# Attention and two feed-forward stages on one core: the product with w_out as seven block products, one written order for all steps, and 29 matmuls in two halves

## The chip, the cores and the metric

The kernel runs on one core of a Trainium2 chip. TensorE (PE, its weight loads PEld), VectorE (DVE), ScalarE (ACT), GpSimd (POOL) and SyncE (SP, which issues the transfers) each work through a queue of their own in order and wait for each other by semaphores. The metric is the time of one execution on the device, in microseconds.

## What is computed

Attention for batch 2, 12 heads, 448 positions, 64 features a head, with a causal mask; its output, 896 tokens of 768 features, goes through two feed-forward stages. The weights arrive as 8-byte floats.

```python
x = attention(q, k, v)              # 896 x 768
g = maximum(x @ w_in, 0) ** 2       # w_in 768 x 2048
y = g @ w_out                       # w_out 2048 x 768
z = maximum(y @ w1, y @ w2, y @ w3) # each 768 x 768
out = z @ moe2_w_out                # 768 x 768
```

## The kernel before

Activations lie transposed: 128 features on the partitions, the 896 tokens in two halves (b = 0, 1, the two batches) of 448 columns. KDM = 6 blocks of 128 features make 768, KFF = 16 make 2048. Every f32 operand is split in two parts of the type fp32r, a rounded high part (`act_hi`, a ScalarE copy, L114) and the low rest (`dve_lo`, a VectorE subtraction, L117). A product of two blocks is three matmuls, high by high, high by low and low by high (`PASSES`), of 448 columns each.

The products with w_in and with w1, w2, w3 go by Winograd's form of Strassen's scheme (`Sevens`): a pair of column blocks of the weight, the two halves of the features and the two token halves make a 2 by 2 block product, done by seven products M1 to M7 in place of eight. Each of the seven is KH = 3 feature blocks by three passes, nine matmuls (L499). The operands are blocks of the activations (a11, a12, a22 and the sums s1 to s4) and of the weights (four blocks and four differences t1 to t4, by VectorE, L124). 8 pairs for w_in (`First`) and 9 for w1 to w3 (`Third`) make 1,071 matmuls. The product with w_out is an ordinary one (`out_slots`): 6 output blocks, 16 feature blocks, three passes, two token halves, 576 matmuls (L627).

A weight block comes by one transfer (`Weight.load`, L152, two buffers `wr`), a ScalarE cast of its upper bits (`cast`, L164) and a VectorE join (`join`, L169), which then issues the next load. `Quarter.hi` and `Quarter.lo` split three 128 by 128 pieces of it into one of five `wq` buffers.

The order of the work has two parts. Attention's twelve pairs of heads, 27 steps of the first weights (`k0` to `k26`) and the first four products (`u0` to `u3`) stand in a text, `ORDER`, one step after the other. Behind it a planner goes through the products as slots: beside each it puts the way out of the product before, the high and low parts of the slot three ahead (`LEAD`), and the weight steps by due times. The squares of the first stage are VectorE instructions (L518, L554).

Steps of the text, with the number of the pair behind the point: `s` scores (L347), `m` masked minimum on VectorE (L358), `e` exponential on ScalarE (L366), `r` reciprocals, `n` normalisation (L378) on POOL, or on VectorE with a stroke (n2'), `g` transposes (L386), `h` their copies to SBUF, on ScalarE, or on VectorE with a stroke, `w` product with v (L417), `xh`, `xl`, `xf`, `d1` to `d4`, `1h` to `4l` operands a and s of the first product. `2l.11` is the low part of s2 for the last pair, the last operand that M6 needs.

Of the kernel before, what the change touches and what calls it, by code (L numbers as in the profile page):

```python
# [32 lines left out]
w3.0 r2.2 n0.1 e5.2 s2.2 n3'.1 s0.3 m2.2 e4.2 m3.2 n2.1 g2.1 m1.3 r0.2 n1.2 e2.2 n6.2 g0.1 e3.2
m0.3 n5.2 h2'.1 g1.1 s2.3 s4.3 n0.2 e1.3 e0.3 m2.3 m3.3 h1.1 n4.2 m4.3 h0'.1 r1.2 s0.4 g3.2 e2.3
m5.3 s6.4 g3.1 xh.0 n2.2 e3.3 xl.0 g2.2 r2.3 n3.2 h3'.1 r1.3 n0.3 h3.2 m1.4 xf.0 s6.3 g0.2 m0.4
m6.3 g1.2 e5.3 w0.1 n3.3 n1.3 e4.3 k0 w1.1 w2.1 w3.1 m6.4 e6.3 s2.4 n2.3 h1.2 h2.2 h0.2 k1 r0.3
e0.4 m2.4 m3.4 n4.3 n5.3 s4.4 m4.4 s2.5 m5.4 e2.4 e6.4 e3.4 e4.4 e1.4 g2.3 n6.3 g1.3 e5.4 d3.1
g0.3 h2'.3 s6.5 m2.5 m3.5 r1.4 g3.3 n2.4 s4.5 m6.5 e2.5 n3.4 r2.4 s0.5 h1.3 w0.2 m4.5 r0.4 m1.5
# [1088 lines left out]
```

## Time and profile before

| | us |
|---|---|
| median of 3 runs | 464.23 (463.86 to 465.28) |
| the profiled execution | 468.29 |
| its span, first to last instruction | 466.5 |
| VectorE busy in the span | 364.3 |
| ScalarE busy in the span | 283.1 |

The profiled execution is one run under the hardware profiler. Durations of single instructions overlap with the start of the next on the same engine; the distance from one start to the next is what an instruction costs in a dense queue. A matmul of two f32 operands that are not split appears as two MATMUL records.

### The profile page before, as it was taken

The numbers are of one execution on the slowest core, as the hardware profiler recorded it, in microseconds if no ns is written. First come the engines' busy times: TensorE is split into PE (matmuls) and PEld (weight loads), VectorE is DVE, ScalarE is ACT, GpSimd is POOL, SyncE is SP. The second block draws the span as 40 slices with busy tenths as digits, with TensorE's granted clock in tenths as the row PEclk, the third lists the DMA queues.
The fourth block names the chain that finished last, engine by engine and source line by source line (L and its number), as shares of the span: only waits on it lengthen the run. The fifth ranks groups of instructions, "written<-read, shape, count | busy, mean of one in ns | idle before, by whom it ended". The sixth has DMA issues, their size and how long they took to land.

```text
span 466.5 us, 6969 instructions
## 1 busy us (share of the span) xinstructions
PE 460.7 (99%) x2434; PEld 402.0 (86%) x2434; DVE 364.3 (78%) x813; ACT 283.1 (61%) x609; POOL 42.4 (9%) x90
## 2 busy tenths in 40 slices
PE   8999999999999999999999999999999999999997
PEld 5766676899999999899999999999999999999996
DVE  5999999998888899992322272898888988898963
ACT  5999999756555557952323254566457656665541
POOL 3656455000000000000000000000000000000000
PEclk9999999999999999999999999999999999999999
DMA  6463543223344441435323423342256466400014
GB/s 214 138 219 127 173 161 91 69 73 112 96 127 136 137 135 45 136 108 186 98 84 112 136 74 111 131 135 68 91 182 197 147 199 203 136 1 1 34 52 152
DMA packets 47619, 56.28 MB, mean 121 GB/s; under 512 B 1761, under 2 KB 43873, under 8 KB 47585
## 3 DMA queue, kind: packets, MB, share of 16 engines
q1 hardware_dynamic: 47296, 55.61, 37.0%
q8 instruction: 19, 0.31, 0.3%
q10 hardware_dynamic: 288, 0.23, 0.2%
q14 instruction: 16, 0.12, 0.1%
HBM read 53.08 MB, written 2.75 MB: 120 GB/s over the span
## 4 chain that ended last, share of the span: by engine, by line
PE 96%; DVE 3%; issue 0%; DVEq 0%
PE ps L499 47%; PE ps L627 26%; PE ps L752 7%; PE ps L347 7%; PE ps L386 4%; PE ps L417 4%; PE ps L1014 1%; PE ps L962 1%; DVE pr L358 1%; DVE s L124 0%; DVE pr L378 0%; DVE a L117 0%; DVE wd L169 0%; DVE st L374 0%; DVE wq L117 0%
## 5 line engine op out<-in xcount | busy, mean ns | idle before, releaser
L499 PE MATMUL ps<-s,wq 128*128 128x448 f32 x612 | 129.6, 368 | 0.0
L499 PEld LDWEIGHTS ps<-s,wq 128*128 128x128 f32 x612 | 114.8, 188 | 11.7 <-ACT s L509 0.2
L499 PE MATMUL ps<-a,wq 128*128 128x448 f32 x459 | 100.0, 370 | 0.0
L627 PE MATMUL ps<-gh,wq 128*128 128x448 f32 x384 | 95.3, 368 | 0.0
L499 PEld LDWEIGHTS ps<-a,wq 128*128 128x128 f32 x459 | 85.5, 188 | 9.0 <-issue 0.4
L117 DVE TENSOR_TENSOR wq<-wd,wq 128x384 fp32r<-128x384 f32 (+1 forms) x87 | 46.0, 533 | 49.3 <-ACT wq L114 45.0
L627 PEld LDWEIGHTS ps<-gh,wq 128*128 128x128 f32 x384 | 72.1, 188 | 7.3
L114 ACT CAST wq<-wd 128x384 fp32r<-128x384 f32 (+1 forms) x87 | 42.9, 499 | 53.8 <-PE ps L627 33.1
L164 ACT CAST up<-wr 128x768 f16<-128x768 bf16 (+1 forms) x58 | 60.8, 1049 | 7.1 <-DMA wr<-in_moe_w 2.1
L169 DVE SCALAR_TENSOR_TENSOR wd<-wr,up 128x768 int32<-128x768 int32 (+1 forms) x58 | 53.8, 928 | 6.1 <-ACT up L164 5.4
L627 PE MATMUL ps<-gl,wq 128*128 128x448 f32 x192 | 55.2, 368 | 0.0
L509 ACT COPY s<-ps 128x448 f32<-128x448 f32 x51 | 27.1, 533 | 37.6 <-PE ps L499 37.1
L366 ACT ACTIVATE pr<-pr,st 128x384 f32<-128x384 f32 (+3 forms) x84 | 44.1, 529 | 5.4 <-DVE st L358 5.2
L117 DVE TENSOR_TENSOR wq<-wt,wq 128x384 fp32r<-128x384 f32 x68 | 37.2, 551 | 9.4 <-ACT wq L114 9.1
L114 ACT CAST wq<-wt 128x384 fp32r<-128x384 f32 x68 | 34.3, 515 | 16.5 <-DVE wt L124 13.4
L378 POOL TENSOR_SCALAR pr<-pr,st 128x256 f32<-128x256 f32 (+3 forms) x77 | 39.9, 534 | 37.6 <-DVE st L374 22.7
L627 PEld LDWEIGHTS ps<-gl,wq 128*128 128x128 f32 x192 | 36.0, 188 | 3.6
L358 DVE CUSTOM_DVE_ANT_0 pr<-ps,mask 128x384 f32<-128x384 f32 (+3 forms) x84 | 34.5, 443 | 5.5 <-PE ps L347 4.9
L347 PE MATMUL ps<-k,q 64*128 64x128 f32 (+3 forms) x168 | 35.5, 445 | 0.0
L386 PEld LDWEIGHTS ps<-ident,pr 128*128 128x128 f32 x192 | 21.6, 140 | 7.5 <-issue 3.1
L386 PE MATMUL ps<-ident,pr 128*128 128x128 f32 x192 | 26.3, 276 | 0.3 <-DVE pr L378 0.3
L124 DVE TENSOR_TENSOR s<-ps,s 128x448 f32<-128x448 f32 (+1 forms) x31 | 18.2, 598 | 9.4 <-ACT s L509 4.5
(108 smaller groups left out, 494.0 us busy)
## 6 DMA issues: line engine op xcount, KB each, us to landing
wr<-in_moe_w_out SPq DMA_DIRECT2D x18, 768.0 KB, 4.3
wr<-in_moe_w SPq DMA_DIRECT2D x18, 768.0 KB, 4.3
wr<-in_moe_w_in SPq DMA_DIRECT2D x16, 768.0 KB, 4.7
v<-in_v SPq DMA_DIRECT2D x12, 256.0 KB, 4.6
wr<-in_moe_w_out SPq DMA_DIRECT2D x6, 512.0 KB, 3.5
q<-in_q SPq DMA_DIRECT2D x11, 256.0 KB, 2.7
out<-s SPq DMA_DIRECT2D x14, 192.0 KB, 1.9
k<-in_k SPq DMA_DIRECT2D x11, 224.0 KB, 2.9
```

The source lines that it names most:

```text
L114: nc.scalar.copy(hi, src)
L117: nc.vector.tensor_tensor(out=lo, in0=src, in1=hi.bitcast(F32), op=SUB)
L164: nc.scalar.copy(self.up.bitcast(FH)[:, :, 1::2], self.top)
L169: nc.vector.scalar_tensor_tensor(out=self.t.bitcast(I32), in0=self.rest, scalar=13, in1=self.up.bitcast(I32), op0=ALU.logical_shift_right, ...
L347: nc.tensor.matmul(sc[:, :keys[w]], self.n["q"][r, w // 2 * P:(w // 2 + 1) * P], self.n["k"][r, :keys[w]], start=True, stop=True,)
L358: nc.vector.tensor_tensor_reduce(out=self.pr[:, offs[u]:offs[u] + n], in0=self.sc[u][:, :n], in1=mask[:, mask.shape[1] - n:], scale=-SCALE ...
L366: nc.scalar.activation(sl, sl, ACTF.Exp, bias=self.st[:, 0, u:u + 1], scale=-1.0, accum_out=self.st[:, 1, u:u + 1],)
L378: engine.tensor_scalar(sl, sl, self.st[:, 2, u:u + 1], 1.0, op0=ALU.mult, op1=ALU.mult)
L386: nc.tensor.transpose(pt[:, i], self.pr[:, offs[u] + kc * P:offs[u] + (kc + 1) * P], shared["ident"])
L499: nc.tensor.matmul(self.acc[n], self.q[n].t[:, ew, i], X[OPERANDS[n]][i][:, ex], start=n in ("M1", "M2", "M5") and i == 0 and e == 0, stop ...
L627: nc.tensor.matmul(acc[b], quarter.t[:, ew, f - k0], (gh, gl)[ex][f][0][:, b], start=f == 0 and e == 0, stop=f == KFF - 1 and e == 2, skip ...
L752: nc.tensor.matmul(acc, a, b, start=start and i == 0 and e == 0, stop=i == KH - 1 and e == 2, skip_group_check=True,)
```

## The change

1. The product with w_out becomes a seven-product scheme as well (`Second`): 8 pairs of feature blocks (j), the two column halves of w_out (l and r, 3 blocks each) and the two token halves. Products run M1, M2, M6, M5, M7, M4, M3, each over j = 0 to 7, three column blocks by three passes. M1 of j 0 to 3 and M3 of j 4 to 7 take one unsplit f32 matmul in place of the three passes (`FULL`). The weight differences (`T1` to `T4`) and activation sums (`S1` to `S4`) are made per j; the activation operand of each product and j is split by `XH` (ScalarE) and `XL` (VectorE). w_out comes in 16 blocks of 768 KB in place of 12 of 768 and 6 of 512.
2. The planner, slots and due times go. `ORDER` now holds 1,693 steps, from the first score to the last results of the w1 to w3 product: `C` cast and `J` join of a weight block, `H` and `L` high and low part of a quarter, `T` differences, `M1` to `M7` products, `V0`, `V1` and so on the way out. The text of attention is another one too: up to `2l.11` it has 25 normalisations on VectorE where the old one has 7 (of 84), 6 joins for 4, 7 `T` steps for 5, 7 `L` steps for 7.
3. In the first and third products, from the third pair on, M1 is copied by ScalarE into the PSUM bank of M2, which adds to it there; VectorE's addition goes (`fresh`). The square of the first stage is done by ScalarE, relu and then square.
4. One matmul in each `Sevens` group (M6, second block, second pass: 17) and 12 in the w_out product are taken as two of 224 columns (`matmul_in_parts`): 29.
5. `st` has three buffers for two. The work behind `ORDER`, with the last product, stays but for how buffers are returned.

```diff
--- before.py
+++ after.py
-LEAD = 3
+FULL = dict(M1=(0, 1, 2, 3), M3=(4, 5, 6, 7))
 RING = 5
 OWN, MORE = 29, 18
-BESIDE = 4
 
 ORDER = """
-s0.0 m0.0 s2.0 m1.0 m2.0 e0.0 s4.0 s6.0 e1.0 m3.0 e2.0 m4.0 e3.0 m5.0 m6.0 s6.1 s0.1 e4.0 r1.0
...
-2l.7 h0.11 3l.9 g1.11 u0.2 1l.7 k23 g2.11 xf.10 u2.2 h1.11 u1.2 h2.11 w0.11 w1.11 k18 k21 k19 k24
-w2.11 k26 k25 w3.11 v1.0 v2.0 u3.0 u3.1 u3.2 d2.11 d4.11 2h.11 d1.11 2l.11 xh.11 4h.11 1h.11 xl.11
-1l.11 4l.11
+s0.0 m0.0 m1.0 s2.0 s4.0 m2.0 e1.0 m3.0 m4.0 s6.0 e0.0 m5.0 e2.0 m6.0 e4.0 e5.0 r2.0 s6.1 s0.1
...
+xh'.7 m6.10 g1.9 g0.9 e2.10 n6.9 xl.7 s4.11 s2.11 h0'.9 3h.5 h1.9 e1.10 m2.11 h2.9 e4.10 C.i3 w0.8
+w1.8 r1.10 m3.11 r2.10 L.f1M2 w2.8 w3.8 g3.9 m5.11 M1a.f0 n2.10 n3'.10 e6.10 g1.10 M1b.f0 m4.11
+e5.10 s6.11 xh.8 d1.7 xl.8 J.i3 H.f1M1 e2.11 M1c.f0 r0.10 n5.10 e5.11 xf.8 h3.9 m6.11 n6'.10 s0.11
+m0.11 w0.9 V0.f0M1 3l.5 e6.11 e3.11 h1.10 m1.11 w1.9 w2.9 e0.11 n1.10 n0'.10 L.f0M2 e4.11 n4.10
+w3.9 g3.10 L.f1M1 M1a.f1 r1.11 1h'.7 g2.10 n2.11 r0.11 n4.11 C.i4 g0.10 n3'.11 h2.10 T1.f0 M2a.f0
+T2.f0 J.i4 e1.11 n6'.11 r2.11 h3.10 n5.11 d3.9 T1.f1 H.f0M6 M1b.f1 M2a.f1 M2b.f0 4l.3 g1.11 g0.11
+n1'.11 L.f0M6 h0.10 w0.10 C.i5 w1.10 J.i5 T2.f1 n0.11 2h.7 T3.f0 w2.10 w3.10 3h.9 h1.11 g3.11
+g2.11 xh.10 xl.10 h0.11 M2b.f1 M2c.f0 M1c.f1 1l.7 h3.11 T3.f1 T1.f2 d4.7 h2.11 xf.10 w0.11 H.f1M6
+2l.7 w1.11 H.f1M3 w2.11 L.f1M6 w3.11 M2c.f1 4h.7 C.i7 L.f1M3 d2.11 2h'.11 V0.f1M1 2l.11 H.f0M7
+4l.7 more d1.11 xh.11 L.f0M7 H.f0M5 J.i7 M6.f0 1h'.11 3l.9 M6.f1 V0.f0M6 1l.11 M7.f0 L.f0M5 H.f1M7
+T4.f0 C.i6 H.f1M5 L.f1M7 L.f1M5 H.f0M4 V0.f1M6 J.i6 C.i11 T4.f1 M5.f0 M5.f1 H.f3M1 d4.11 L.f0M4
+4h.11 M7.f1 V0.f1M2 V0.f0M7 V1.f1M2 J.i11 xl.11 H.f1M4 V0.f1M7 T1.f3 V2.f1M2 L.f1M4 M4.f0 L.f3M1
...
+T3.o1 V1.f4M3 T2.o1 M3.f6 V1.f6M2 V0.f6M3 V0.f7M2 H.o3M2 S2.o2 L.o3M2 M3.f7 V0.f7M4 J.o3r V1.f7M4
+V1.f6M4 S4.o1 V2.f4M3 V1.f7M2 M1.o2 L.o6M1 M2.o0 V0.f7M3 XH.o6M1 XL.o4M6 S1.o1 XH.o1M7 V1.f6M3
+H.o1M2 XL.o6M1 C.o4r M1.o3 H.o4M1 V2.f6M7 J.o4r L.o4M1 T1.o4 M1.o4 XH.o0M5 V2.f6M3 L.o1M2 M2.o1
...
+WL.5 Z4.l V.2
...
-                self.st = att.tile([P, 3, 2 * NQ + 1], F32, tag="st", name="st")
+                self.st = att.tile([P, 3, 2 * NQ + 1], F32, tag="st", name="st", bufs=3)
...
+    def matmul_in_parts(acc, w, x, at, **flags):
+
+        for c in (slice(0, at), slice(at, S)):
+            if c.start < S:
+                nc.tensor.matmul(acc[:, c], w, x[:, c], skip_group_check=True, **flags)
...
+                    matmul_in_parts(
                         self.acc[n], self.q[n].t[:, ew, i], X[OPERANDS[n]][i][:, ex],
-                        start=n in ("M1", "M2", "M5") and i == 0 and e == 0,
-                        stop=i == KH - 1 and e == 2, skip_group_check=True,
+                        S // 2 if (n, i, e) == ("M6", 1, 1) else S,
+                        start=n in self.starts and i == 0 and e == 0, stop=i == KH - 1 and e == 2,
...
         def e1(self):
-            return [lambda: self.keep("s1")], []
+            if self.fresh:
+                return [lambda: self.keep("s1")]
+            return [lambda: nc.scalar.copy(self.d, self.b)]
...
+        def relu(self, f, b, acc=None):
+            o = unit_of(g, "g", f, b, 2)
+            nc.scalar.activation(o, o if acc is None else acc, ACTF.Relu)
+
+        def square(self, f, b):
+            o = unit_of(g, "g", f, b, 2)
+            nc.scalar.activation(o, o, ACTF.Square)
+
+        def squared(self, f, b, acc=None):
+
+            return [lambda: self.relu(f, b, acc), lambda: self.square(f, b)]
 
         def c11(self):
             o = self.fa, 0
-            return [lambda: self.added(*o, self.d, "s1")], [lambda: square(unit_of(g, "g", *o))]
+            if self.fresh:
+                return [lambda: self.added(*o, self.d, "s1"), *self.squared(*o)]
+            return self.squared(*o, self.d)
...
+    class Second:
+
+
+        B = [ps[i][:, :S] for i in (6, 7, 0)]
+        C = [ps[i][:, :S] for i in (2, 4, 3)]
+        HALF = KH * P
+
+        X_AT = dict(M1=(0, 0), M2=(1, 0), M5=(0, 0), M7=(0, 1), M4=(1, 1), M3=(1, 0))
+
+        W_AT = dict(M1=(0, 0), M2=(0, 1), M5=(0, 0), M7=(1, 0), M4=(0, 1), M3=(1, 1))
...
+        def t_1(self, j):
+            dve(self.wt("M5", j), self.wt("M7", j), self.wt("M1", j), SUB)
+
+        def t_2(self, j):
+            t = self.t2[j] = s_tile()[:, :self.HALF].rearrange("p (m c) -> p m c", c=P)
+            dve(t, self.wt("M3", j), self.wt("M5", j), SUB)
+
+        def t_3(self, j):
+            dve(self.wt("M7", j), self.wt("M3", j), self.wt("M7", j), SUB)
+
+        def t_4(self, j):
+            dve(self.wt("M4", j), self.wt("M2", j), self.t2[j], SUB)
+
+        def s_3(self, j):
+            dve(self.g(j, 0, 1), self.g(j, 0, 0), self.g(j, 0, 1), SUB)
+
+        def s_2(self, j):
+            k = "pair", j // 2
+            if k not in self.s2:
+                self.s2[k] = Kept("s2", 6, (2, S))
+            self.s2[j], self.s2[j, "kept"] = self.s2[k].t[:, j % 2], self.s2[k]
+            dve(self.s2[j], self.g(j, 1, 1), self.g(j, 0, 1), SUB)
+
+        def s_1(self, j):
+            dve(self.g(j, 0, 0), self.s2[j], self.g(j, 0, 0), ADD)
+            self.s2[j, "kept"].used()
+
+        def s_4(self, j):
+            dve(self.g(j, 1, 0), self.g(j, 1, 0), self.s2[j], SUB)
+            self.s2[j, "kept"].used()
+
+        def x_hi(self, n, j):
+            self.x[n, j] = units.take("x")
+            act_hi(self.x[n, j][0][:, 0], self.xt(n, j))
+
+        def x_lo(self, n, j):
+            t = self.x[n, j][0]
+            dve_lo(t[:, 1], self.xt(n, j), t[:, 0])
+            self.x_used(n, j)
+
...
+        def acc(self, n, m):
+            return (self.C if n in ("M2", "M5", "M3") else self.B)[m]
+
+        def flags(self, n, j, first, last):
+            return dict(
+                start=n in ("M1", "M2", "M5") and j == 0 and first, stop=j == NI - 1 and last,
+            )
+
+        def run(self, n, j):
+            (x, key), q = self.x[n, j], self.q[n, j]
+            for m in range(KH):
+                for e, (ew, ex) in enumerate(PASSES):
+                    matmul_in_parts(
+                        self.acc(n, m), q.t[:, ew, m], x[:, ex],
+                        S // 2 if (j % 4, m, e) == (0, 1, 1) else S,
+                        **self.flags(n, j, e == 0, e == 2),
+                    )
+            units.give(key)
+
+        def run_full(self, n, j):
+            for m in range(KH):
+                nc.tensor.matmul(
+                    self.acc(n, m), self.wt(n, j)[:, m], self.xt(n, j), skip_group_check=True,
+                    **self.flags(n, j, True, True),
                 )
-
-                def run(quarter=quarter, k0=k0 + r0, k1=k0 + r1):
-                    for f in range(k0, k1):
-                        for e, (ew, ex) in enumerate(PASSES):
-                            for b in range(B):
-                                nc.tensor.matmul(
-                                    acc[b], quarter.t[:, ew, f - k0], (gh, gl)[ex][f][0][:, b],
-                                    start=f == 0 and e == 0, stop=f == KFF - 1 and e == 2,
-                                    skip_group_check=True,
-                                )
-                    if m == KDM - 1:
-                        for f in range(k0, k1):
-                            units.give(gh[f][1])
-                            units.give(gl[f][1])
-
-                res.append(Slot(run, quarter, None, (m, k0 + r0)))
-
-        def evac():
-            if m == KDM - 1:
-                shared["y"] = acc
-                return [], []
-            y[m] = units.take(f"y{m}", F32)
-            return [lambda b=b: nc.scalar.copy(y[m][0][:, b], acc[b]) for b in range(B)], []
-
-        res[-1].evac = evac
-        return res
-
-    blocks_o = [Weight(w_o, f, 1, 0, DM) for f in range(KF2)]
+            self.used(n, j)
+            self.x_used(n, j)
+
+        def out(self, n):
+            def at(m, h, b):
+                return unit_of(y, "y", m + h * KH, b, 2 + h)
+
+            def kept(h, b):
+                return [lambda m=m: nc.scalar.copy(at(m, h, b), self.B[m]) for m in range(KH)]
+
+            def added(h, b):
+                return [lambda m=m: dve(at(m, h, b), self.C[m], at(m, h, b), ADD) for m in range(KH)]
+
+            return dict(
+                M1=kept(0, 0), M2=added(0, 0), M6=kept(1, 0), M5=[], M7=kept(1, 1) + added(1, 1),
+                M4=kept(0, 1), M3=added(1, 0),
+            )[n]
...
```

## Rows read from the trace of the kernel before

**Rows 1.** Page, busy time by engine, then groups: line engine op, out<-in, count, busy, mean ns

```profile
span 466.5 us, 6969 instructions
...
PE 460.7 (99%) x2434; PEld 402.0 (86%) x2434; DVE 364.3 (78%) x813; ACT 283.1 (61%) x609; POOL 42.4 (9%) x90
...
L378 POOL TENSOR_SCALAR pr<-pr,st 128x256 f32<-128x256 f32 (+3 forms) x77 | 39.9, 534 | 37.6 <-DVE st L374 22.7
...
L386 PE MATMUL ps<-ident,pr 128*128 128x128 f32 x192 | 26.3, 276 | 0.3 <-DVE pr L378 0.3
```

**Rows 2.** Windows, attention and each product: from:to, length, busy by engine, clock, DMA

```profile
10.00:91.10 81.10, 80.77 (x570) 56.33 (x570) 78.23 (x298) 75.34 (x232) 39.45 (x76) 1.00 0.45 145
91.10:186.00 94.90, 94.90 (x461) 86.13 (x460) 82.51 (x149) 55.37 (x99) 0.00 (x0) 1.00 0.35 106
186.00:306.00 120.00, 120.00 (x582) 108.77 (x581) 63.84 (x102) 57.05 (x98) 0.00 (x0) 1.00 0.35 115
306.00:420.00 114.00, 114.00 (x554) 103.52 (x553) 101.52 (x186) 70.04 (x126) 0.00 (x0) 1.00 0.42 138
420.00:466.50 46.50, 43.05 (x244) 42.16 (x242) 33.32 (x63) 20.06 (x42) 0.00 (x0) 1.00 0.17 60
```

**Rows 3.** Chain of waits in order of time, from 88 us: start, us, what

```profile
88.73 95.08 PE ps L499 x459
183.81 3.65 PE ps L627 x18
187.46 2.03 PE ps L499 x9
189.49 3.72 PE ps L627 x18
193.21 1.86 PE ps L499 x9
195.07 111.60 PE ps L627 x540
306.67 113.46 PE ps L499 x549
...
434.77 28.30 PE ps L752 x162
```

**Rows 4.** Timeline of PE, 183 to 188 us: start, us, what

```profile
183.64 0.57 PE L627 MATMUL ps<-gh,wq 128*128 128x448 f32 x2
...
186.89 0.57 PE L627 MATMUL ps<-gh,wq 128*128 128x448 f32 x2
```

**Rows 5.** Timeline of the weight loads, 181 to 188 us

```profile
181.72 0.90 PEld L499 LDWEIGHTS ps<-s,wq 128*128 128x128 f32 x5 [0.18 <-ACT s L509]
...
187.35 0.71 PEld L499 LDWEIGHTS ps<-a,wq 128*128 128x128 f32 x4 [0.28 <-ACT s L509]
```

**Rows 6.** Timeline of PE, three places in attention

```profile
42.54 0.92 PE L347 MATMUL ps<-k,q 128*128 128x448 f32 x2
43.30 1.04 PE L386 MATMUL ps<-ident,pr 128*128 128x128 f32 x8
...
76.44 0.60 PE L386 MATMUL ps<-ident,pr 128*128 128x128 f32 x4
...
90.62 7.60 PE L499 MATMUL ps<-s,wq 128*128 128x448 f32 x36
```

**Rows 7.** Timeline of VectorE, three places

```profile
70.88 0.68 DVE L378 TENSOR_SCALAR pr<-pr,st 128x256 f32<-128x256 f32 x1
71.48 0.15 DVE L373 TENSOR_SCALAR st<-st 128x2 f32<-128x2 f32 x1
...
81.20 0.34 DVE L378 TENSOR_SCALAR pr<-pr,st 128x256 f32<-128x256 f32 x1
81.46 0.38 DVE L443 CAST s<-s 128x448 fp32r<-128x448 f32 x1
...
90.51 0.62 DVE L117 TENSOR_TENSOR s<-s,s 128x448 fp32r<-128x448 f32 x1
91.05 0.62 DVE L117 TENSOR_TENSOR a<-ps,a 128x448 fp32r<-128x448 f32 x1
...
97.50 0.55 DVE L117 TENSOR_TENSOR wq<-wd,wq 128x384 fp32r<-128x384 f32 x1
97.97 0.55 DVE L124 TENSOR_TENSOR wt<-wd 128x384 f32<-128x384 f32 x1
...
98.97 0.95 DVE L169 SCALAR_TENSOR_TENSOR wd<-wr,up 128x768 int32<-128x768 int32 x1
99.84 0.55 DVE L117 TENSOR_TENSOR wq<-wt,wq 128x384 fp32r<-128x384 f32 x1
```

**Rows 8.** Timeline of ScalarE, high halves of two weight quarters

```profile
102.15 0.51 ACT L114 CAST wq<-wt 128x384 fp32r<-128x384 f32 x1
102.57 0.51 ACT L114 CAST wq<-wd 128x384 fp32r<-128x384 f32 x1
```

**Rows 9.** Page, DMA issues: count, KB each, us to landing

```profile
wr<-in_moe_w_in SPq DMA_DIRECT2D x16, 768.0 KB, 4.7
```

**Rows 10.** Timeline of POOL, 69 to 83 us

```profile
70.45 3.33 POOL L378 TENSOR_SCALAR pr<-pr,st 128x384 f32<-128x384 f32 x6 [2.84 <-DVE st L373]
78.19 2.68 POOL L378 TENSOR_SCALAR pr<-pr,st 128x384 f32<-128x384 f32 x5 [4.41 <-DVE st L374]
```

More of the change, by code (lines that the diff above doesn't have):

```diff
@@ L33 @@
[L33 to L38, printed above, removed]
@@ L124, in dve, with load_next @@
         nc.vector.tensor_tensor(out=o, in0=a, in1=b, op=op)
+    todo, blocks, line = {}, {}, []
+    def load_next():
+        if line:
+            line.pop(0).load()
     class Kept:
@@ L660, in tile_attention_moe_moe, with c12, c21 @@
[L660 to L664 removed]
+            return [
+                lambda: self.keep("s3"), lambda: self.added(self.fb, 1, self.c, "s3"),
+                *self.most(self.fb, 1, "s3"),
+            ]
+        def c12(self):
+            return [lambda: self.added(self.fb, 0, self.c, "s2"), *self.most(self.fb, 0, "s2")]
+        def c21(self):
+            return [lambda: self.whole(self.fa, 1, self.b)]
@@ L839, in way_out @@
-    def way_out(n):
-        prior = slots[n - 1] if n else None
-        return prior.evac() if prior is not None and prior.evac else ([], [])
-    def beside(n):
-        before, late = way_out(n)
-        if n in urgent:
-            before = before + [urgent[n]]
-        for step in before + weight_steps(n) + late + extra.get(n, []):
-            step()
-        units.settle()
-    def convert(f):
-        t, key = g[f]
-        gh[f], gl[f] = units.take(f"gh{f}"), units.take(f"gl{f}")
-        hi_lo(gh[f][0], gl[f][0], t)
-        units.give(key)
@@ L992, in tile_attention_moe_moe @@
-    more = ctx.enter_context(tc.tile_pool(name="more", bufs=1))
-    units.add(more, MORE, "m")
-    for e in range(2):
-        todo[f"v{BESIDE - 1}.{e}"]()
-    for n in range(BESIDE, len(slots)):
-        slots[n].run()
-        beside(n)
-    before, late = way_out(len(slots))
-    for step in before + late:
-        step()
+    own = ExitStack()
+    att = own.enter_context(tc.tile_pool(name="att", bufs=2))
+    constants(att)
+    prs = [att.tile([P, offs[-1]], F32, name=f"pr{n}", bufs=1) for n in range(PR)]
@@ new lines, in tile_attention_moe_moe, with more_units @@
+    warm = att.tile([P, 2 * P], FR, name="warm", bufs=1)
+    nc.vector.memset(warm.bitcast(F32), 0.0)
+    for _ in range(WARM):
+        nc.tensor.matmul(ps[7][:, :2 * P], warm[:, :P], warm, start=True, stop=True)
+    for t in prs:
+        nc.gpsimd.memset(t[:, offs[-2] + S:], 0.0)
+    def more_units():
+        own.close()
+        units.add(ctx.enter_context(tc.tile_pool(name="more", bufs=1)), MORE, "m")
+    todo["wload"], todo["more"] = load_next, more_units
+    for i in range(B * NP):
+        todo |= Pair(i).steps()
@@ new lines, in tile_attention_moe_moe @@
+    order = ORDER.split()
+    line += [blocks[n[2:]] for n in order if n.startswith("C.")]
+    for i in range(3):
+        todo[f"load.{i}"]()
+        if i:
+            todo[f"loadv.{i - 1}"]()
+    done = set()
+    for n in ORDER.split():
+        assert n not in done or n == "wload", n
+        done.add(n)
+        todo[n]()
+        step, *i = n.split(".")
+        if step == "s0" and int(i[0]) + 3 < B * NP:
+            todo[f"load.{int(i[0]) + 3}"]()
+        if step == "w0" and int(i[0]) + 2 < B * NP:
+            todo[f"loadv.{int(i[0]) + 2}"]()
```

586 lines of the change are left out of this document (281 added, 305 removed).

## The prediction

> **What bounds the kernel now.** I read the page's busy line first [rows 1]: PE is busy 99% of the span, but that share can't be taken as it stands, because matmuls overlap in the records. The table by stretches [rows 2] splits the run into attention (to 91.1 us), the product with w_in (to 186), the product with w_out (to 306), the products with w1 to w3 (to 420) and the last product. The reader is to see two regimes. In attention VectorE is busy 78.23 of 81.10 us and ScalarE 75.34, so VectorE sets the pace. From 91.1 to 420 PE never stops, while VectorE falls as low as 63.84 of 120 us beside w_out. The granted clock is 1.00 (the 2.4 GHz level) in every stretch.
>
> The chain of waits [rows 3] confirms it: from 88.73 us on it is PE's own matmuls, piece after piece, so a matmul removed there shortens the end by its start distance, as long as the other two engines keep up. The w_out product is three pieces, 18 + 18 + 540 matmuls: 3.65 + 3.72 + 111.60 = 118.97 us. The large piece gives 111.60/540 = 206.7 ns per matmul of 448 columns; the third product's piece, 113.46/549, gives the same.
>
> **The w_out product.** Before: 576 matmuls, 118.97 us. After: 8 pairs of feature blocks, 7 products, 3 column blocks, 168 places. 144 of them take three passes, 432 matmuls: 432 x 206.7 ns = 89.3 us. The other 24 (M1 of j 0 to 3, M3 of j 4 to 7) are unsplit f32. Such a matmul appears as two MATMUL records; the unsplit 448-column score starts at 42.54 and PE's next work at 43.30 [rows 6], so 0.76 us each, 24 x 0.76 = 18.2 us. (Three passes would be 0.62 us: these 24 cost PE 3.3 us and spare the other engines the splitting.) Sum 107.5 us: **11.4 us less** on the path that sets the end.
>
> **The 29 split matmuls.** No row has 224 columns with this operand type. Lower bound: the line through 448 columns (206.7) and 384 (28.30/162 = 174.7 ns) [rows 3] reaches 95 ns at 224, so a split would give back 17 ns, 0.5 us in all. Upper bound: each half costs what 384 columns do, so 143 ns more per split, 4.1 us. Nearest for a short matmul with its own weight load are the transposes of 128 columns, four in 0.60 us with 276 ns taken by one, so (0.60 - 0.28)/3 = 0.11 us apart [rows 1, 6]; I take 115 ns a half, 23 ns more per split, **+0.7 us**. The Trainium skill ("TensorE: Matmul & The Clock Gate", Back-to-back issue gap) gives N/2.4 + 2.5 ns: for 448 columns 189 ns, where this trace has 206.7, so the measurement decides; by that page, as an estimate, the 29 splits would cost under 0.1 us.
>
> **Two paces.** The same 448-column matmul also runs at another distance. Between 183.64 and 186.89 us 16 matmuls start, 203 ns each [rows 4], and this holds from one wait of the weight loads (0.18 us at 181.72) to the next (0.28 us at 187.35) [rows 5]; behind the second the pace is 206.7 again for the rest of the stage. The clock is the same, so the pace looks like a state that a jolt in the stream of loads can set, and it then lasts. A split is a jolt: two loads where one was, one in 51 of the remaining matmuls. Lower bound 0; upper bound all 1,467 remaining three-pass matmuls (1,035 of the first and third products, 432 here) at 203: 1,467 x 3.6 ns = 5.3 us. One jolt of two led to the faster pace; I take half, **-2.6 us**.
>
> **Attention, in the new order.** M6.f0 is the first product for which attention must be over; it waits for VectorE's step `2l.11`. Before, it starts at 90.62 us [rows 6], and the step is the 448-column difference at 90.51 [rows 7]. I count VectorE's steps up to `2l.11` in both orders. A step costs the distance to the next start in dense work [rows 7]: 448 columns 0.54 us (90.51 to 91.05), 384 columns 0.47 (97.50 to 97.97), a join 0.87 (98.97 to 99.84). New: 18 more normalisations on VectorE (25 for 7), 2 more joins (6 for 4) +1.7, 2 more T differences +0.9, one more placement +0.5; fewer copies of x and sums on VectorE -1.8; `d1`, `d4`, `3l.9`, `4l.7` moved behind -2.2. A normalisation of 256 columns took 0.26 us (81.20 to 81.46) where POOL was idle and 0.60 (70.88 to 71.48) where POOL ran the same operation beside it [rows 7, 10]. So 18 cost between 4.7 and 10.8 us, and the whole is +3.8 to +9.9 us. POOL was busy 39.45 of 81.1 us [rows 2] and loses 18 of its 77 normalisations [rows 1], so most new ones should find it idle; and VectorE had 2.9 us idle that another order may fill. I take **+5 us**. The Trainium skill ("SBUF — State Buffer", Who interferes with whom) says that VectorE in a two-port mode and GpSimd share a port pair and that whoever issues second is fully blocked; the pair 0.26 and 0.60 agrees.
>
> **Who must keep up behind it.** Behind `2l.11` I count, with the same prices, 278 us of VectorE work to the end of the order against 326 us of PE work, and 212 us of ScalarE (0.42 us for a high half) [rows 8]. The squares go from VectorE to ScalarE, whose 57.05 of 120 us leave room. So the cover for all new T, S, XH and XL steps is PE's own stream; without it each would cost its 0.47 to 0.54 us. But one stretch is tight. From M2.o0 to M4.o0 (M2, M6, M5, M7 of w_out) VectorE has 69 L and XL steps, 30 T, 15 S, 9 joins and 6 others, 67.5 us, against 69.2 us of matmuls, and at M2.o0 it can be ahead by little: the last results of the w_in product, which it handles in that place, leave PE only one product, M1.o2 (2.3 us), before it. VectorE did 101.52 of 114 us (89%) beside a full PE [rows 2], where it had no need of more. Bounds: 0 (it keeps up, with that lead) and 67.5/0.89 - 69.2 = 6.6 us. I take **+1.5 us**, nearer to zero because it reached 96% in attention, where it was needed.
>
> **Loads.** Per block SP issues one transfer, as before, behind the join that frees the buffer; two buffers, 4.7 us to landing [rows 9]. Eight blocks of the left half must now be decoded by the end of the w_in product. From each join to the cast two blocks later I count the matmuls in the order: mostly 5.6 us and more; 1.9 for `i13`, 2.3 for `b2`, 3.7 for four others. There ScalarE waits up to 2.8 us, with high halves for products some five places later queued behind it. I take nothing, since ScalarE is at two thirds; without that cover 2.8 us each.
>
> **Sum.** The profiled execution took 468.29 us with a span of 466.5; the median of the runs is 464.23, 0.9% less, and both get the same differences. -11.4 + 0.7 - 2.6 + 5 + 1.5 = -6.8: 464.2 - 6.8 = **457.4 us**. All low ends together: -11.4 - 0.5 - 5.3 + 3.8 = -13.4, 450.8, or 448 if VectorE's idle 2.9 us in attention are filled too; all high ends: -11.4 + 4.1 + 9.9 + 6.6 = +9.2, 473.4.
>
> **Rivals.**
> 1. The fast pace holds nearly everywhere. For: it lasted until the next wait. Against: one jolt of two ended it. 457.4 - 2.7 = 454.7; with a good attention order 450. Chance 0.20.
> 2. The splits do nothing for the pace, and attention costs its full 9.9: 464.2 - 11.4 + 0.7 + 9.9 + 1.5 = 464.9, no change that can be measured (0.3%, 1.4 us, is about what a measurement of this kernel can tell). For: VectorE is at 96% there. Against: POOL has less to do. Chance 0.08.
> 3. The other side: VectorE becomes the bound. One mechanism, its steps at the upper prices above: 0.60 us for a normalisation up to `2l.11`, and 89% at most between M2.o0 and M4.o0, where PE then waits for XL steps. 464.2 - 11.4 + 0.7 + 9.9 + 6.6 = 470.0, slower. It decides once VectorE's delays together pass 11.4 - 0.7 + 1.4 = 12.1 us. For: 98% load in that stretch. Against: attention's 96%, and the order places most XL steps well ahead of their products. Chance 0.12.
> 4. The change doesn't do what it says: seven products for eight bring nothing, because 24 unsplit f32 matmuls cost more than 0.76 us. It would take 1.2 us each; no row speaks for that. Under 0.02, counted with 3.
>
> **Numbers.** Forecast (452 to 462) 0.60, rival 1 0.20, rival 2 0.08, rival 3 with 4 0.12. Faster: 0.60 + 0.20 and a quarter of rival 2, 0.82; the same 0.06; slower 0.12. Range 449 to 464.5: it leaves out the slow end of rivals 2 and 3 and the best end of rival 1.
>
> **What would show it.** The w_out matmuls in about 107 us plus any waits; pieces of the chain at 203 and at 207 ns, and a change of pace at a split; M6.f0 starting at 94 to 97 us instead of 90.6; VectorE above 94% beside M2 to M7 of w_out, ScalarE near two thirds. Wrong, if PE idles for VectorE by more than 3 us there, if M6.f0 starts before 91 or after 101, or if the pace is below 200 or above 210 ns.

## The result, and the profile after

The changed kernel takes 458.54 us (median of 4 runs, 457.79 to 459.29); the kernel before, in the same series, 464.52 (463.86 to 465.28). The ratio is 0.9857, 95% interval 0.9816 to 0.9898: faster by 6.0 us (1.4%). 457.4 was forecast, in a range of 449 to 464.5. The profiled execution took 458.93 us, with a span of 457.1.

The page's busy line, in the form of [rows 1]:

```profile
PE 447.7 (98%) x2367; PEld 385.1 (84%) x2367; DVE 396.3 (87%) x900; ACT 324.3 (71%) x712; POOL 35.2 (8%) x72
```

VectorE works 32 us more than before, ScalarE 41 us more, and the end still comes earlier: most of it lies beside PE. The table by stretches, with the columns of [rows 2]: attention, the products with w_in, w_out and w1 to w3, the last product, and then the tight stretch from M2.o0 to M4.o0:

```profile
10.00:94.70 84.70, 82.29 (x567) 56.36 (x567) 82.18 (x309) 78.81 (x237) 32.69 (x59) 1.00 0.51 157
94.70:187.80 93.10, 92.38 (x460) 84.22 (x459) 75.82 (x136) 78.07 (x150) 0.00 (x0) 1.00 0.59 170
187.80:298.70 110.90, 110.90 (x520) 95.51 (x519) 108.18 (x203) 79.67 (x153) 0.00 (x0) 1.00 0.36 108
298.70:418.40 119.70, 119.44 (x597) 109.74 (x596) 98.26 (x181) 66.34 (x126) 0.00 (x0) 1.00 0.26 85
418.40:457.10 38.70, 34.73 (x199) 34.09 (x197) 26.95 (x53) 16.59 (x36) 0.00 (x0) 1.00 0.20 72
197.80:266.30 68.50, 68.50 (x342) 62.54 (x341) 67.03 (x129) 49.40 (x96) 0.00 (x0) 1.00 0.34 104
```

The table shows two things. Beside w_out VectorE is busy 108.18 of 110.90 us, and in the tight stretch 67.03 of 68.50 (98%), with PE busy all the time. And attention is longer: 84.7 us from 10 us on, where it was about 80.6 [rows 2, 6].

The chain of waits, in order of time (start, us, what), to be held against [rows 3]:

```profile
150.62 4.43 DMA wr<-in_moe_w_out
155.13 1.07 ACT up L250
...
160.12 27.82 PE ps L558 x137
187.94 4.51 PE ps L814 x12
192.45 3.64 PE ps L558 x18
196.09 2.25 PE ps L814 x6
...
202.44 78.64 PE ps L558 x397
...
301.41 5.70 DMA wr<-in_moe_w
...
310.46 92.21 PE ps L558 x457
```

L558 is a three-pass matmul, L814 an unsplit f32 one (two records each): a product of three takes 2.25 us, 0.75 us each. The large piece holds 377 whole matmuls and the 20 halves of ten split ones; 78.64/387 = 203 ns each, where [rows 3] had 206.7. The timeline of PE gives the start of M6.f0:

```profile
94.70 4.47 PE L558 MATMUL ps<-s,wq 128*128 128x448 f32 x23
```

94.70 us, where [rows 6] had 90.62.

### The profile page after: what moved, and what is told of

Read it like the earlier page. It is cut to its first block, busy times and chain, and to the rows that moved or that the text cites. A ratio compares the mean times of both kernels' runs of the same rounds, so it can differ in the third digit from the quotient of the medians.

```text
span 457.1 us, 6969 instructions
## 1 busy us (share of the span) xinstructions
PE 447.7 (98%) x2367; PEld 385.1 (84%) x2367; DVE 396.3 (87%) x900; ACT 324.3 (71%) x712; POOL 35.2 (8%) x72
## 4 chain that ended last, share of the span: by engine, by line
PE 53%; DVE 9%; DMA 2%; ACT 2%; issue 0%; ACTq 0%; SPq 0%
PE ps L558 46%; PE ps L989 5%; PE ps L814 2%; DVE z L202 1%; DMA wr<-in_moe_w 1%; DVE y L202 1%; DVE piece L195 1%; DVE wd L202 1%; DVE wd L255 1%; DMA wr<-in_moe_w_out 1%; DVE s L195 1%; ACT up L250 1%; ACT wq L192 1%; DVE s L202 0%; DVE z2l L195 0%
## 5 line engine op out<-in xcount | busy, mean ns | idle before, releaser
L558 PE MATMUL ps<-s,wq 128*128 128x448 f32 (+1 forms) x629 | 130.1, 362 | 0.6 <-ACT ps L596 0.6
L558 PEld LDWEIGHTS ps<-s,wq 128*128 128x128 f32 x629 | 115.1, 188 | 11.1 <-ACT ps L596 1.0
L558 PE MATMUL ps<-a,wq 128*128 128x448 f32 x459 | 101.6, 370 | 0.7 <-ACT wq L192 0.3
L558 PEld LDWEIGHTS ps<-a,wq 128*128 128x128 f32 x459 | 85.2, 188 | 10.3 <-DVE wq L195 0.8
L558 PE MATMUL ps<-x,wq 128*128 128x448 f32 (+1 forms) x444 | 89.0, 362 | 0.0
L558 PEld LDWEIGHTS ps<-x,wq 128*128 128x128 f32 x444 | 81.5, 188 | 6.9 <-issue 0.6
L250 ACT CAST up<-wr 128x768 f16<-128x768 bf16 x56 | 60.2, 1075 | 12.0 <-DMA wr<-in_moe_w_in 3.8
L192 ACT CAST wq<-wd 128x384 fp32r<-128x384 f32 x91 | 46.0, 511 | 26.3 <-PE ps L558 26.1
L255 DVE SCALAR_TENSOR_TENSOR wd<-wr,up 128x768 int32<-128x768 int32 x56 | 53.7, 959 | 9.4 <-ACT up L250 9.4
L195 DVE TENSOR_TENSOR wq<-wd,wq 128x384 fp32r<-128x384 f32 x91 | 49.0, 551 | 9.3 <-ACT wq L192 9.0
L440 ACT ACTIVATE pr<-pr,st 128x128 f32<-128x128 f32 (+3 forms) x84 | 44.0, 528 | 6.9 <-DVE st L432 6.6
L432 DVE CUSTOM_DVE_ANT_0 pr<-ps,mask 128x128 f32<-128x128 f32 (+3 forms) x84 | 34.8, 444 | 4.5 <-PE ps L421 4.2
L421 PE MATMUL ps<-k,q 64*128 64x384 f32 (+3 forms) x168 | 36.0, 446 | 1.5 <-DVE st L432 1.3
L591 ACT COPY s<-ps 128x448 f32<-128x448 f32 x38 | 20.0, 529 | 12.7 <-PE ps L558 11.4
```

The lines of the kernel that those rows point to most:

```text
L192: nc.scalar.copy(hi, src)
L195: nc.vector.tensor_tensor(out=lo, in0=src, in1=hi.bitcast(F32), op=SUB)
L250: nc.scalar.copy(self.up.bitcast(FH)[:, :, 1::2], self.top)
L255: nc.vector.scalar_tensor_tensor(out=self.t.bitcast(I32), in0=self.rest, scalar=13, in1=self.up.bitcast(I32), op0=ALU.logical_shift_right, ...
L421: nc.tensor.matmul(sc[:, :keys[w]], self.n["q"][r, w // 2 * P:(w // 2 + 1) * P], self.n["k"][r, :keys[w]], start=True, stop=True,)
L432: nc.vector.tensor_tensor_reduce(out=self.pr[:, offs[u]:offs[u] + n], in0=self.sc[u][:, :n], in1=mask[:, mask.shape[1] - n:], scale=-SCALE ...
```

## The experiments

Every series held runs of the kernel before as well. Times are medians; "changed" is the changed kernel, 458.54 us in its first series and 458.29 in e11. Where a run is set against the changed kernel of another series, the ratios to the kernel before give the same difference to within some 1 us (e5 7.2, e6 2.4, e7 6.3 us).

### e1 and e2: the changed kernel without the splits, the kernel before with them

```diff
-    S // 2 if (n, i, e) == ("M6", 1, 1) else S,
+    S,
...
-    S // 2 if (j % 4, m, e) == (0, 1, 1) else S,
+    S,
```

e2 does the reverse in the kernel before: 17 splits in its `Sevens`, 12 in its w_out product.

> The changed kernel with all 29 split matmuls whole again, nothing else. Theory (the splits keep PE at the short distance): the dense stretches go back from 203 to 206.7 ns a matmul wherever no wait happens to jolt them, so up to 1,467 x 3.8 ns = 5.6 us longer, less the 29 x 0.02 = 0.6 us that the splits themselves cost: 460 to 464 us. Rival (the pace comes from the new order or the new operands, not from the splits): the pace stays at 203 and the kernel gets 0.3 to 0.6 us faster, 458.

> The kernel before with 29 matmuls taken as two of 224 columns (M6, second block, second pass in each seven-product group; 12 in the w_out product), nothing else. Theory: its 1,611 dense matmuls behind 90 us go from 206.7 to 203 ns, 6 us shorter against the kernel before wherever that runs at 206.7: ratio 0.987 to 0.990. Rival (the pace does not come from the splits): 0.3 to 0.6 us slower, ratio 1.001.

Measured: e1 457.43 us (456.76 to 458.61), ratio to before 0.9838 (0.9805 to 0.9871). e2 462.98 (462.29 to 463.49), ratio 0.9953 (0.9933 to 0.9972). So splits alone make the kernel before a little faster, and the change needs none of them. The pace shows it. In e1 the chain has a piece of three-pass matmuls at 203 ns (87.56/432) and one in which they are 207 ns apart from 309 to 397 us:

```profile
201.03 87.56 PE ps L558 x432
...
297.61 104.44 PE ps L558 x504
```

In e2 it is 203 from the first split at 91.7 us on; its first piece has 451 whole matmuls and 16 halves, 93.63/459 = 204, its piece of w_out 529 and 22, 109.64/540 = 203:

```profile
88.97 93.63 PE ps L502 x467
...
193.72 109.64 PE ps L633 x551
```

The same first piece takes 95.08 us without splits, in e4 below, where PE stays at 207 ns from 89 to 181 us. The splits inside the traces say why. In e11, the changed kernel once more, PE runs at 207 ns from a wait of its weight loads at 159 us (0.39 us) on:

```profile
164.91 5.74 PE L558 MATMUL ps<-a,wq 128*128 128x448 f32 x27
170.49 3.85 PE L558 MATMUL ps<-s,wq 128*128 128x448 f32 x20
174.18 1.98 PE L558 MATMUL ps<-a,wq 128*128 128x448 f32 x9
```

From 164.91 to 170.49 it is 5.58/27 = 207 ns, from 174.18 to 176.00, where the next piece starts, 1.82/9 = 202; the split at 171.3 lies between. In the eleven traces with splits, 13 splits have 207 ns (206.0 to 206.8) in the matmuls before them; behind all 13 it is 203 (202.5 to 203.5), and behind no split is it 207. So a split ends the slow pace. It is not the only thing that does, as e1 shows: there the fast one is reached at 96.3 us, beside a wait of the loads of 0.06 us, and again at 397.

A split costs next to nothing: the 11 here take 0.20 us more than the same piece of e4 without them, 18 ns each.

### e4: the kernel before once more

> The kernel before, unchanged, for a second profile. Theory (the pace is a state that a chance wait sets): the stretches at 203 and 206.7 ns may lie elsewhere than in the first profile, and the span differs by up to 6 us with them; the runs shown before, with a median of 464.2, lie 4 us under the first profiled execution, which ran at 206.7 nearly throughout. Rival: the same paces at the same places, ratio 1.000 and a span near 466.

Measured: 464.90 us (463.84 to 467.79), ratio 1.0017 (0.999 to 1.0044). The profiled execution has a span of 462.3, not 466.5, and the reason stands in the chain: the first piece is as slow as in [rows 3], 95.08/459 = 207, and from the next wait of the weight loads (0.18 us at 181.24) on the pace is 203:

```profile
88.26 95.08 PE ps L499 x459
183.34 3.65 PE ps L627 x18
...
194.44 109.44 PE ps L627 x540
303.88 60.46 PE ps L499 x297
```

The same program, another pace: the profile on which the prediction rested was an execution at the slow one nearly throughout.

### e3: the normalisations shared out as before

```diff
-s0.2 r0.1 m4.2 m1.2 m0.2 h2.0 w0.0 n4.1 e2.1 w1.0 e6.2 m5.2 n5.1 w2.0 e1.2 n1'.1 n6'.1 w3.0 e4.2
+s0.2 r0.1 m4.2 m1.2 m0.2 h2.0 w0.0 n4.1 e2.1 w1.0 e6.2 m5.2 n5.1 w2.0 e1.2 n1.1 n6.1 w3.0 e4.2
```

(one line of `ORDER`; 18 strokes fewer in all)

> The changed kernel with the normalisations divided between POOL and VectorE as in the kernel before (7 of 84 on VectorE instead of 25), at the same places of the order. Theory (VectorE sets the end of attention, a normalisation costs it 0.26 to 0.6 us): M6.f0 starts 4.7 us or more earlier, at 90 us or before, and the kernel is 3 to 5 us faster. Rival (POOL's latency is what the new assignment takes off the path): M6.f0 starts no earlier or up to 5 us later, since 18 more of 0.5 us each stand in POOL's queue.

Measured: 457.49 us (456.73 to 458.06), ratio 0.9833 (0.9801 to 0.9865); M6.f0 at 94.04, only 0.66 us earlier. The stretch from 10 to 90 us, first the changed kernel, then e3 (engines in the order PE, PEld, VectorE, ScalarE, POOL):

```profile
10.00:90.00 80.00, 77.77 (x540) 53.44 (x540) 77.48 (x300) 74.65 (x228) 32.69 (x59) 1.00 0.51 156
```

```profile
10.00:90.00 80.00, 77.35 (x544) 52.73 (x542) 74.42 (x287) 75.42 (x232) 42.59 (x77) 1.00 0.50 158
```

VectorE is relieved by 3 us and attention gets almost nothing of it: VectorE alone does not set this pace.

### e5 and e8: weight steps behind `2l.11`, alone and with e3

```diff
-2l.7 w1.11 H.f1M3 w2.11 L.f1M6 w3.11 M2c.f1 4h.7 C.i7 L.f1M3 d2.11 2h'.11 V0.f1M1 2l.11 H.f0M7
-4l.7 more d1.11 xh.11 L.f0M7 H.f0M5 J.i7 M6.f0 1h'.11 3l.9 M6.f1 V0.f0M6 1l.11 M7.f0 L.f0M5 H.f1M7
...
+2l.11 H.f0M7 4l.7 more d1.11 xh.11 L.f0M7 H.f0M5 C.i4 J.i4 M6.f0 1h'.11 3l.9 M6.f1 V0.f0M6 1l.11
+M7.f0 L.f0M5 T3.f1 C.i5 H.f1M7 J.i5 T4.f0 H.f1M5 L.f1M7 L.f1M5 C.i7 J.i7 H.f0M4 V0.f1M6 T1.f2
+T4.f1 M5.f0 M5.f1 C.i6 J.i6 C.i11 H.f3M1 d4.11 L.f0M4 4h.11 M7.f1 V0.f1M2 V0.f0M7 V1.f1M2 J.i11
```

> Steps C and J of i4 and i5, C and J of i6 and i7, C.i11, T1.f2 and T3.f1 stand behind 2l.11 here, nothing else changes. Theory: the later start of M6.f0 (94.70 us for 90.62) is due to weight work moved ahead of 2l.11; 2 joins and 2 T on VectorE cost about 2 x 0.87 + 2 x 0.47 = 2.7 us there and 3 casts on ScalarE about 0.9 us, so M6.f0 starts at 91.5 to 92.7 us and, as PE has eight products ahead of the moved steps, the kernel takes 2 to 3 us less than the changed one, about 456. Rival: VectorE and ScalarE share the work of attention so evenly that taking these steps away moves M6.f0 by under 1 us, as with the normalisations; then the kernel stays at 457.5 to 458.5. Second rival: the casts and joins come too late behind it, PE waits for weights within 110 to 130 us, and the time rises above 459.

> The moved weight steps of the run before it in this list together with the normalisations as they were shared out before (7 on VectorE). Theory: either alone leaves the other engine as the limit of attention (VectorE or ScalarE); together M6.f0 starts at 90.5 to 92 us and the kernel takes 3 to 4 us less than the changed one, 454 to 455. Rival: the sum of the two single effects, M6.f0 at 92 to 93.5 us, or no more than with the normalisations alone (94.0, 457.5 us).

Measured: e5 466.35 us (464.80 to 468.02), ratio 1.0012 (0.9984 to 1.004), 8 us slower than the changed kernel; e8 465.56 (464.70 to 467.37), ratio 0.9993 (0.9966 to 1.0021). M6.f0 starts at 94.44 and 93.21 us. The second rival came out, 7 us above the 459 it named. The chain of e5:

```profile
97.22 0.87 DVE wd L257
...
98.12 4.80 DMA wr<-in_moe_w_in
...
103.00 1.08 ACT up L252
...
104.10 0.97 DVE wd L257
...
105.09 4.55 DMA wr<-in_moe_w_in
...
110.63 0.50 ACT wq L194
111.13 0.47 ACT s L519
111.60 0.44 ACT s L593
```

A join (L257) issues the next load; a join that is moved moves a load. The cast (L252) waits for it on ScalarE, and behind the cast, in the same queue, stands the copy (L593) that empties the PSUM bank for PE's next product. PE idles 5.07 us, and then its clock has fallen. e5 by stretches: the idle one, and 3.7 us of dense matmuls behind it:

```profile
106.50:112.10 5.60, 0.53 (x4) 0.16 (x2) 3.80 (x6) 2.95 (x6) 0.00 (x0) 0.82 0.89 265
```

```profile
112.50:116.20 3.70, 3.70 (x11) 3.27 (x11) 3.51 (x8) 2.99 (x7) 0.00 (x0) 0.50 0.73 213
```

A granted clock of 0.50 is the 1.2 GHz level. Matmuls of 448 columns start 373 ns apart there, 203 from 117 us on; the dozen slow ones cost 2 us more. The Trainium skill ("TensorE: Matmul & The Clock Gate", Wait — 56ns, not 53.3ns?) gives N/1.2 ns for a cold array, 373 for 448 columns: the trace agrees.

### e6: w_out without the matmuls of M6

```diff
-            for m in range(KH):
+            for m in range(0 if n == "M6" else KH):
```

> Leaves out the matmuls of product M6 of w_out (72 matmuls, 8 x 1.825 = 14.6 us of PE); their operands are still made. Theory: VectorE kept up between M2.o0 and M4.o0 with its 67.0 of 68.5 us because PE set the pace; with 14.6 us of PE gone VectorE (no slack left) becomes the bound: the stretch shrinks by little, at most by 4 us unless VectorE runs ahead of PE by more than that when M2.o0 starts; the kernel then takes 1 to 6 us less than the changed one, PE waiting for XL, S and T steps. Rival: VectorE works well ahead of PE, so its busy share only mirrors free buffers; then the whole 14.6 us come off, about 444 us.

Measured: 457.14 us (456.27 to 457.71), ratio 0.9805 (0.9754 to 0.9857). 14.6 us of PE work taken out bring 1.4 us. M2.o0 to M4.o0 lasts 67.4 us (197.59 to 264.97), where it lasted 68.4. e6 by stretches:

```profile
215.00:225.00 10.00, 7.32 (x38) 6.46 (x36) 10.00 (x21) 7.84 (x18) 0.00 (x0) 1.00 0.00 0
225.00:235.00 10.00, 9.05 (x34) 7.26 (x35) 10.00 (x21) 6.33 (x13) 0.00 (x0) 0.83 0.48 159
235.00:245.00 10.00, 6.67 (x21) 5.41 (x20) 10.00 (x20) 6.34 (x13) 0.00 (x0) 0.72 0.24 78
```

VectorE is busy 30.00 of 30 us and PE waits for it. In the changed kernel it was 1 to 1.5 us away from making PE wait: 1.0 by this comparison, in which PE's clock fell as well (0.72 and 0.83), and 1.5 by its idle time there (67.03 of 68.50).

### e7: the square back on VectorE

```diff
-            nc.scalar.activation(o, o, ACTF.Square)
+            nc.vector.scalar_tensor_tensor(out=o, in0=o, scalar=0.0, in1=o, op0=ALU.max, op1=ALU.mult)
```

The relu stays on ScalarE only where it is also the copy out of PSUM.

> The square of the first stage goes back to VectorE (max with 0, times itself, one instruction of 896 or 448 columns), ScalarE keeps the copies only. 32 units of 448 columns at 0.54 us and more, 17 us of VectorE work, most of it before M2.o0. Theory: VectorE had 17 us idle between 100 and 186 us and takes it, but comes to M2.o0 later and has no room to catch up in the stretch to M4.o0: 2 to 6 us slower than the changed kernel, 460 to 464. Rival: it keeps the lead it needs, no change (458 to 459), and moving the squares to ScalarE was not needed.

Measured: 464.93 us (464.40 to 467.16), ratio 0.9993 (0.9965 to 1.0022): the whole gain is gone, 6.5 us. Behind M2.o0:

```profile
203.90:213.00 9.10, 5.52 (x17) 4.64 (x16) 9.06 (x18) 2.08 (x4) 0.00 (x0) 0.64 0.41 139
```

VectorE comes to the tight stretch late and PE pays twice, 3.6 us of waiting at once and a clock of 0.64 (part of the stretch at the 1.2 GHz level). So moving the squares to ScalarE, which belongs to part 3 of the change, is a condition of its gain.

### e10: M3 of j 4 to 7 in three passes

```diff
-FULL = dict(M1=(0, 1, 2, 3), M3=(4, 5, 6, 7))
+FULL = dict(M1=(0, 1, 2, 3))
```

(with `H`, `L`, `XH`, `XL` for these four in the order, the operands of M3.o0 ahead of those of M3.o2, and three `H` of the next stage behind M3.o3)

> M3 of j 4 to 7 of w_out in three passes in place of one unsplit f32 matmul: 36 matmuls at 203 ns for 12 at 752 ns, PE 1.7 us less; ScalarE gets 8 high parts and VectorE 8 low parts more (4 us each engine), just behind the stretch in which VectorE had 67.0 of 68.5 us. Theory: VectorE has no slack there, so PE waits for XL of these products by more than it gains: 0 to 3 us slower than the changed kernel, 458.5 to 461. Rival: there is slack behind M4.o0, 1.7 us come off, about 457.

Measured: 464.18 us (462.57 to 466.11), ratio 0.9953 (0.9924 to 0.9982), 5.9 us above the changed kernel beside it. e10 by stretches:

```profile
299.00:306.50 7.50, 4.36 (x17) 2.94 (x17) 7.30 (x13) 4.82 (x9) 0.00 (x0) 0.88 0.63 210
```

PE waits 1.4 us for an `XL` at 288 and some 4 us between 298.7 and 306, with VectorE busy 7.30 of 7.50. The theory's sign is right, the loss twice the upper end of what was expected. Its mechanism, a wait for `XL`, is shown for the 1.4 us alone: the longest wait behind it, 2.1 us, ended with a ScalarE copy (L595), and the moved steps have an unknown share in it.

### e9, e11 and e12: attention in the old order

The steps of attention stand as in the `ORDER` of before, the weight steps `k0` to `k26` and the first products under their new names. Behind them, e9:

```diff
+2h.11 d1.11 2l.11 H.f1M6 L.f1M6 xh.11 4h.11 1h.11 xl.11 1l.11 4l.11 more M6.f0 M6.f1 V0.f0M6
+C.i4 M7.f0 T3.f1 J.i4 H.f1M7 T4.f0 C.i5 H.f1M5 L.f1M7 J.i5 L.f1M5 H.f0M4 V0.f1M6 T4.f1 M5.f0
+M5.f1 T1.f2 L.f0M4 H.f1M3 L.f1M3 M7.f1 C.i7 V0.f1M2 V0.f0M7 V1.f1M2 J.i7 H.f1M4 V0.f1M7 V2.f1M2
+L.f1M4 M4.f0 C.i6 V1.f0M7 J.i6 H.f3M1 T1.f3 L.f3M1 T2.f3 C.i11 J.i11 C.i9 V1.f1M7 H.f2M1 L.f2M1
...
```

e12 against e9:

```diff
-L.f1M4 M4.f0 C.i6 V1.f0M7 J.i6 H.f3M1 T1.f3 L.f3M1 T2.f3 C.i11 J.i11 C.i9 V1.f1M7 H.f2M1 L.f2M1
...
+L.f1M4 H.f2M1 L.f2M1 T2.f2 H.f2M6 M4.f0 V1.f0M7 V1.f1M7 T4.f2 L.f2M6 M4.f1 V0.f0M4 C.i6 V0.f1M4
+J.i6 H.f3M1 T1.f3 L.f3M1 M1.f2 C.i11 T2.f3 M1.f3 V0.f2M1 J.i11 H.f3M5 H.f0M3 V0.f0M2 T4.f3
+L.f3M5 V1.f0M2 L.f0M3 V0.f3M1 M3.f1 V0.f1M3 H.f2M2 T3.f2 M6.f2 C.i9 L.f2M2 H.f3M6 L.f3M6 M5.f3
...
```

> The changed kernel with the steps of attention in the order of the kernel before: 7 normalisations on VectorE, 4 joins, the same four products beside it; the weight steps that the new text had ahead of 2l.11 follow behind M6.f0, the casts two or more products apart. Theory: the 4.1 us by which M6.f0 starts later are the order of attention as a whole (neither the normalisations, 0.66 us, nor the weight steps, 0.26 us, explained them); M6.f0 starts at 90.2 to 91.2 us, and the kernel takes 2.5 to 4 us less than the changed one, 454.5 to 456, as long as PE does not wait for the later weights. Rival: what attention leaves out comes back: PE waits for joins and loads behind M6.f0 by 2 to 4 us, and the time is 457.5 to 459. Second rival: three buffers of st or the loads hold attention, not the order; M6.f0 stays at 93 to 95.

> The changed kernel as it is, for its own spread and as the base of the two runs beside it: 457.8 to 459.3 us, PE at 203 ns for 448 columns nearly everywhere, M6.f0 at 94.4 to 95.0 us. If the pace of PE is a matter of the execution alone, the pieces at 203 and 207 ns lie elsewhere than in the first execution.

Measured: e11 458.29 us (457.58 to 460.56), ratio 0.9838 (0.9788 to 0.9887), M6.f0 at 94.76. e9 462.84 (462.55 to 464.01), ratio 0.9931 (0.9902 to 0.996), 4.5 us above e11. M6.f0 starts 3.5 us earlier, and PE loses more than that behind it. Timeline of PE, then the chain of e9:

```profile
91.27 2.02 PE L560 MATMUL ps<-s,wq 128*128 128x448 f32 x10
```

```profile
98.07 6.41 DMA wr<-in_moe_w_in
...
104.56 1.09 ACT up L252
...
105.67 0.97 DVE wd L257
...
106.65 4.81 DMA wr<-in_moe_w_in
...
111.54 1.05 ACT up L252
112.59 0.37 ACT wq L194
112.96 0.45 ACT g L620
```

```profile
PE ps L560 <- ACT g L620: 7.2, 1, 7.2
```

It is e5's pattern: load, cast, and behind the cast the relu that frees a bank (L620), for which PE idles 7.2 us (the last line, from the list of PE's waits). e12 puts the casts of i6, i11, i9, i10 and i8 one to five products later (i7 stays).

> As the run with attention in the old order, but behind M6.f0 each cast of a weight block stands where its load has landed (two buffers, each load issued by a join, 4.8 us to landing): casts of i7, i6, i11, i9, i10, i8 two to five products later, and the copies out of PSUM that the next product needs ahead of them. Theory: the 9.1 us that PE lost there came from ScalarE standing in a cast that waits for a load, with the copy that frees the PSUM bank queued behind it; without that wait PE does not stop between M6.f0 (91.3 us) and 125 us, and 3.5 us of attention are kept: 454 to 455.5 us, faster than the changed kernel. Rival: the loads themselves are too late, whatever the order of the casts: PE waits for weights by 3 to 7 us behind 100 us, 458 to 462.

In e12 the copy of M1.f2 stands ahead of the addition that reads f0's M2 from the same bank, so one block of g gets other values; the work is the same, but the wait between these two is turned round. Measured: 458.22 us (457.25 to 458.43), ratio 0.9842 (0.9804 to 0.9879): no faster than the changed kernel. M6.f0 starts at 91.08 us, but from there to M1.o0 it takes 95.8 us where e11 takes 92.2. What PE loses at 106 to 110 us has shrunk to 1.6 us; another 2.6 us stand at 131 to 135, from the next loads, this time by way of VectorE:

```profile
127.37 5.41 DMA wr<-in_moe_w_in
...
132.85 1.08 ACT up L252
...
133.96 0.96 DVE wd L257
134.92 0.55 DVE g L204
```

So the rival holds for these two orders. Whether some order keeps the 3.5 us is open.

## Why the prediction was right, point by point

The time was right, 457.4 for 458.5, and the largest term, the pace and the tight stretch were right in mechanism. Attention was right in size and had another cause, and the misses of the single terms, up to 1.5 us each, cancelled: that the sum came this close was in part luck. The profile of before ran at the slow pace nearly throughout, so I compare e11 with e4, whose spans (456.2 and 462.3) are those of usual runs:

| term | predicted | measured, e11 against e4 |
|---|---|---|
| w_out product, without its splits | -11.4 | 116.7 to 105.6: -11.1 |
| 29 splits | +0.7 | +0.5 (18 ns each, e2 against e4) |
| pace | -2.6 | -1.5 (some 380 matmuls more at the fast pace x 4 ns) |
| attention, start of M6.f0 | +5 | 90.15 to 94.76: +4.6 |
| tight stretch | +1.5 | 0 |
| loads | 0 | +0.7 (waits of PE beside w_in and w1 to w3, 1.6 us for 0.9) |
| last product | none | +0.6 (38.2 to 38.8) |
| sum | -6.8 | -6.2; the spans differ by 6.1 |

**w_out.** Right. 48 three-pass products took 87.8 us with their 12 splits (0.2 us), and the eight unsplit ones 18.0, 2.25 each; in e4 the product of before ran at 203 ns too, so the term is free of the pace. An f32 matmul was priced at 0.76 us; 0.75 was measured. Rival 4 is out.

**Pace.** Right that there are two, that the faster one would prevail, and that a split is a jolt that sets it: a change of pace at a split, one of the signs that the prediction named, is there in 13 places. The prediction gave a jolt one chance in two; every split that met the slow pace ended it, so in the changed kernel the pace fell back only here and there (207 ns at 160 to 171 us in e11), until the next split. The splits are not needed for it, though: e1 has none, reaches the fast pace without them and is as fast as the changed kernel. And one step failed outright, that "both get the same differences": the profiled 468.29 was all slow pace, while usual runs of before have the fast one in part, so most of what the profile promised there was not to be had from the median. Rival 1 described the changed kernel's pace well and its time, 454.7, badly, for that reason, and the term is 1.5 us in place of 2.6. It varies with the executions of before: beside e11, where these have a median of 467.12 us, the changed kernel is 8.8 us faster.

**Attention.** The size fits (+4.1 in the first profile, +4.6 here); the account does not. I charged it to VectorE's steps, the normalisations above all. VectorE's busy time up to M6.f0 did grow by about what I counted, 77.73 to 82.18 us, but taking 18 normalisations off it brought 0.66 us (e3), taking the moved weight steps off 0.26 (e5), both 1.5 (e8). Only the whole old order brings 3.5 (e9); which of its steps do it, and what the other 1.1 us are, stays open. With VectorE, ScalarE and PE all above 92% busy, no single engine's sum prices this stretch. What the prediction did not see is what the 4 us buy: joins taken earlier, and with them the next loads. Without that, PE gives the time back behind attention (e5, e9, e12).

**The tight stretch.** Priced at 67.5 us of VectorE for 69.2 of PE; it was 67.03 for 68.50, and PE did not wait, so the 1.5 us charged were too much. e6 shows that the busy share hid no slack: with PE's work cut, the stretch still took 67.4 us. Any microsecond more would have counted, though rival 3's whole price of 12 us was far off. e7 shows it at work: 16 us more for VectorE, 24 of the 32 squares ahead of M2.o0, cost 6.5.

**Loads.** I had ScalarE wait and PE not. It is a mild miss here: ScalarE waited 3.8 us for w_in's loads in the first profile, PE less than 1 us more than before. "Without that cover 2.8 each" was too low by far, because I left out the queue: a late cast holds the copies out of PSUM behind it, and after 5 to 7 us idle (e5, e9) PE came back at half its clock, 0.50 in e5.

## What to carry to other kernels

A step that issues a load is worth more than its own duration: moving it later moves the load, the cast that waits for it, and everything queued behind that cast, above all a copy that frees a PSUM bank. Where two engines are both near full, take a stage's work out of one of them to see how much room the other has; the busy shares alone don't say. And where a matmul's distance differs by 2% between stretches, compare several executions before a profile's own span is taken for the usual one.
